# Expert loop with a gated layer behind it: weight conversions and sums issued with lags of steps, in three to four buffers

## The chip, the cores and the metric

One core of a Trainium2 chip runs the program alone. The metric is the device time of one execution in microseconds, the median of the runs. TensorE is PE in the profile (PEld: its weight loads), VectorE is DVE, ScalarE is ACT, GpSimd is POOL, SyncE is SP, which issues nearly all DMAs. PEclk is the granted TensorE clock.

## The reference, cut to what matters

```python
x = attention(q, k, v, f_logit)           # (3072, 384), gated linear attention
# experts: one per token (argmax of the logits), 8 experts, 384 -> 1024 -> 384
for e in range(8):
    h = np.maximum(x[mask] @ w1[e], 0.0)
    out[mask] = gate_w[mask, None] * (h @ w2[e])
x = out
# gated layer, 384 -> 1536 -> 384
a = x @ w_a
b = x @ w_b
return (a * b @ w_out).astype(np.float32)
```

`w_a`, `w_b` and `w_out` arrive as 64-bit floats.

## The kernel before, in words

The program has three stages: attention, the loop over the experts, and the gated layer. All instructions are placed by hand in one program order (each engine takes its own list in order), with the waits on data added by the framework.

**The expert loop** runs steps `s = 0..63` (`NE * FJ`, eight experts of eight blocks of 128 hidden columns). Tokens are sorted by expert; expert 0 has 224 tokens left here, the others 448 down to 384 columns (`CAPS`). A float32 product is three matmuls on a high and a low part (`mm3`). A step has `h_part(s)`: nine matmuls into `ph`, then the Relu `hh` on ACT (L1157) and the low part `hl` on DVE (L1158); and `y_part(s - 1)`: nine matmuls with `hh` and `hl` of the step before into `po` (L1177). After an expert's last block `po` goes to `yT` at an offset known at run time (L1193, L1195). Steps 3 to 5 of each expert turn the next expert's rows (`x_turn`, L1124 to L1128, 84 transposes in the loop). `w_more(s)` runs the jobs that load (`job_load`, L876) and split the expert weights: high part on ACT (L890), low part two thirds on POOL and one third on DVE (L893); two raw tiles, six split tiles.

**The preparation of the gated layer's weights** lies in the same loop. `prep_run(us)` takes operations from one generator, `prep()`, until a credit in us is used, 1.0 per step up to step 7 and 1.5 then; what is left at the last step runs there at once. It has two kinds of work:

- `conv(todo)` turns a piece of a 64-bit weight (768 KB) to float32 with integer operations: a load into `raws` (L910, two buffers in the tile `big`, one piece ahead), Abs on ACT (L916), two tensor_scalars on DVE (L938, L939), then L942 and L947 or L951. Pieces of `w_out` are then split into a high and a low part (L921, L922) and stored to `wost` (L927).
- `combine(w)` keeps the float32 weight of `w_a` or `w_b` in DRAM (`wkeep`, L962) and forms `NR = 15` blocks of 128 x 512, eight of them sums of up to two operations on DVE (L964, L965). For each block: high part on ACT (L1006) and low part on POOL (L1007) into one of two `hilo` buffers, the next block's sums, then the store of the block before to `wst` (L1000). The gated layer multiplies with these fifteen blocks in place of the original ones.

The order is six pieces of `w_out`, six of `w_a`, the sums of a, six of `w_b`, the sums of b. All of it, the converted weight `wf` too, lies in `big` (9216 columns). After step 63 `w_chunk(0..2)` loads the first chunks of `wst`.

**The gated layer** has 392 slots `at`: each a `visit` with six matmuls per block pair on a chunk (L1386), evictions on ACT and DVE (L1389 to L1402), a product and its split (L1363 to L1368), and the output matmuls `pq` with `w_out` (L1415 to L1419), whose pieces `wo_load` reads from `wost` three ahead, in the order 0, 8, 4, 1, 9, 5, 2, 10, 6, 3, 11, 7. Chunks are asked for every four slots, two ahead (`w_chunk(at // 4 + 2)`, L1017).

Of the kernel before, what the change touches and what calls it, by code (L numbers as in the profile page):

```python
# [46 lines left out]
NR = 15  # L47
# [9 lines left out]
def build(tc, I, out, dbg=None):  # L57
# [93 lines left out]
    with tc.manual_schedule():  # L151
# [716 lines left out]
        loaded = []  # L868

        def job_load(s):  # L870
# [28 lines left out]
        hilo_o = big[:, 7680:9216].bitcast(F32R).rearrange("p (i j d) -> p i j d", i=2, j=2)  # L899
# [3 lines left out]
        def conv_load(n, w, c):  # L903
            raw = raws[n % 2].bitcast(I32)
# [5 lines left out]
            SP.dma_start(out=raw.rearrange("p (k f) -> p k f", k=src.shape[1]), in_=src)  # L910

        def conv(todo):
            halves = lambda n: [raws[n % 2].bitcast(I32).rearrange("p (f two) -> p f two", two=2)[:, :, i] for i in range(2)]

            def start(n):
                A.activation(out=ct.bitcast(F32), in_=halves(n)[1].bitcast(F32), func=ACTF.Abs)  # L916

            def rest(n):
                c = todo[n][1]
                src = halves(n)[0].bitcast(F32).rearrange("p (j d) -> p j d", j=2)  # L920
                A.activation(out=hilo_o[:, 0], in_=src, func=ACTF.Copy)  # L921
                G.tensor_tensor(out=hilo_o[:, 1], in0=src, in1=hilo_o[:, 0].bitcast(F32), op=ALU.subtract)  # L922

            def store(n):
                c = todo[n][1]
                for i in range(2):
                    SP.dma_start(out=wost[2 * c:2 * c + 2, :, i].rearrange("j p d -> p j d"), in_=hilo_o[:, i].bitcast(F32))  # L927

            last = lambda n, w: 0 <= n < len(todo) and todo[n][0] == w
            conv_load(0, *todo[0])  # L930
            yield 1.5
            yield 1.5
            start(0)
            for n, (w, c) in enumerate(todo):
                if n + 1 < len(todo):
                    conv_load(n + 1, *todo[n + 1])
                r0, r1 = halves(n)
# [5 lines left out]
                if last(n - 1, 2):  # L943
                    store(n - 1)
                yield 0.95
                if w == 2:
                    V.scalar_tensor_tensor(out=r0, in0=r1, scalar=-1073741824, in1=r0,  # L947
                                           op0=ALU.bitwise_and, op1=ALU.bitwise_xor)
                else:
                    as3 = lambda t: t.rearrange("p (k f) -> p k f", k=KC)  # L950
                    V.scalar_tensor_tensor(out=wf.bitcast(I32)[:, :, c * 256:(c + 1) * 256], in0=as3(r1), scalar=-1073741824,  # L951
                                           in1=as3(r0), op0=ALU.bitwise_and, op1=ALU.bitwise_xor)
                if n + 1 < len(todo):
                    start(n + 1)
                if w == 2:
                    rest(n)
                yield 0.95
            if last(len(todo) - 1, 2):
                store(len(todo) - 1)

        def combine(w):
            SP.dma_start(out=wkeep[w], in_=wf)  # L962
            blk = lambda m, k: wf[:, k, m * 512:(m + 1) * 512]
            two = lambda out, x, y, op=ALU.subtract: V.tensor_tensor(out=out, in0=x, in1=y, op=op)  # L964
            neg = lambda out, x, y: V.scalar_tensor_tensor(out=out, in0=x, scalar=-1.0, in1=y, op0=ALU.mult, op1=ALU.subtract)  # L965
            T0, T1 = tmps
            plan = (
                (14, blk(0, 2), ()),
                (8, blk(0, 1), ()),
                (13, T0, ((two, T0, blk(0, 1), blk(1, 0)),)),  # L970
                (0, blk(1, 0), ()),
                (9, T1, ((two, blk(0, 2), blk(0, 2), blk(0, 0)), (two, T1, blk(1, 0), blk(0, 2)))),
                (3, blk(2, 0), ()),
                (11, blk(0, 2), ((two, blk(0, 2), blk(0, 2), blk(2, 0)),)),
                (6, blk(1, 2), ()),
                (4, blk(0, 0), ((two, blk(0, 0), blk(0, 0), blk(0, 1)), (two, blk(0, 0), blk(0, 0), blk(2, 0), ALU.add))),
# [5 lines left out]
                (2, T0, ((two, T0, blk(0, 2), blk(1, 2), ALU.add), (two, T0, T0, blk(2, 2), ALU.add))),  # L982
            )

            def sums(i):
                if i < NR:
                    for op, *args in plan[i][2]:
                        op(*args)
                    return 0.7 * max(1, len(plan[i][2]))
                return 0.3  # L990

            def store(i):
                late, half, pos = AT[plan[i][0]]
                src = hilo[i % 2].bitcast(F32).rearrange("p t i c -> p t (i c)")
# [7 lines left out]
            yield sums(0)  # L1002
            for i in range(NR):
                as4 = lambda t: t.rearrange("p (t c) -> p t c", t=4)
                src, to = as4(plan[i][1]), hilo[i % 2]
                A.activation(out=to[:, :, 0], in_=src, func=ACTF.Copy)  # L1006
                G.tensor_tensor(out=to[:, :, 1], in0=src, in1=to[:, :, 0].bitcast(F32), op=ALU.subtract)  # L1007
                cost = sums(i + 1)
                if i:
                    store(i - 1)  # L1010
                yield cost
            store(NR - 1)
# [6 lines left out]
        def prep():  # L1019
            yield from conv([(2, c) for c in range(6)] + [(0, c) for c in range(6)])  # L1020
            yield from combine(0)
            yield from conv([(1, c) for c in range(6)])
            yield from combine(1)

        prep_ops = prep()
        credit = [0.0]

        def prep_run(us):
            credit[0] += us
            while credit[0] > 0:  # L1030
                try:
                    credit[0] -= next(prep_ops)
                except StopIteration:
                    credit[0] = -1e9
# [253 lines left out]
        for s in range(NE * FJ):  # L1288
# [67 lines left out]
        def wo_load(n):  # L1356
            if n < NQF:
                SP.dma_start(out=WO[n % 4].bitcast(F32), in_=wost[fseq(n)[1]])
# [101 lines left out]
        for at in range(8 * (NTT * NU + 1)):  # L1460
# [237 lines left out]
```

## Time and profile before

| | |
|---|---|
| median of 3 runs | 928.13 us (927.87 to 934.37) |
| the execution in the profile | 922.55 us, its span 920.8 us |
| PE, DVE, ACT, POOL busy | 790.6, 601.2, 418.8, 412.6 us |
| granted TensorE clock, mean | 0.943 of full |
| DMA | 231.54 MB, mean 251 GB/s |

The span goes from the first to the last instruction. Busy shares are means over the three stages, which have different limits; a stage is read from windows of its own: a row of a window has its start and end, its length, the busy us of each engine with its instructions in brackets, then the granted clock, the busy share of the DMA engines and the rate. Steps are found in the trace by the Relu (L1157), one per step.

### The profile page before, as it was taken

The numbers are of one execution on the slowest core, as the hardware profiler recorded it, in microseconds if no ns is written. First come the engines' busy times: TensorE is split into PE (matmuls) and PEld (weight loads), VectorE is DVE, ScalarE is ACT, GpSimd is POOL, SyncE is SP. The second block draws the span as 40 slices with busy tenths as digits, with TensorE's granted clock in tenths as the row PEclk, the third lists the DMA queues.
The fourth block names the chain that finished last, engine by engine and source line by source line (L and its number), as shares of the span: only waits on it lengthen the run. The fifth ranks groups of instructions, "written<-read, shape, count | busy, mean of one in ns | idle before, by whom it ended". The sixth has DMA issues, their size and how long they took to land.

```text
span 920.8 us, 16764 instructions
## 1 busy us (share of the span) xinstructions
PE 790.6 (86%) x6354; PEld 753.4 (82%) x6354; DVE 601.2 (65%) x993; ACT 418.8 (45%) x889; POOL 412.6 (45%) x394
## 2 busy tenths in 40 slices
PE   7999999878676474887655999999999999999996
PEld 5899899767665473887544999999999999999995
DVE  7999974876555353576481776676676676676652
ACT  5999945543434242534341353443443343443431
POOL 6667843554224453444351252452452452552423
PEclk8999999999979677999786999999999999999998
DMA  7988628787645646654758888987988988988982
GB/s 273 347 280 285 232 96 243 231 265 236 182 146 182 186 128 188 194 199 177 175 146 290 317 304 295 328 315 287 342 301 291 333 299 290 333 307 295 332 307 101
DMA packets 83328, 231.54 MB, mean 251 GB/s; under 512 B 10634, under 2 KB 42232, under 8 KB 76712
## 3 DMA queue, kind: packets, MB, share of 16 engines
q1 hardware_dynamic: 79879, 220.81, 70.8%
q0 software_dynamic: 3072, 9.56, 2.7%
q8 instruction: 52, 0.85, 0.4%
q14 instruction: 37, 0.30, 0.1%
q10 hardware_dynamic: 288, 0.02, 0.0%
HBM read 192.95 MB, written 37.42 MB: 250 GB/s over the span
## 4 chain that ended last, share of the span: by engine, by line
PE 42%; DVE 21%; DMA 13%; issue 13%; POOL 6%; ACT 3%; SPq 1%; ACTq 0%; DVEq 0%; POOLq 0%
PE pv L1386 19%; DMA wst<-big 7%; PE pw L1386 5%; PE pq L1419 4%; PE pq L1415 4%; PE pq L1417 4%; POOL w L893 4%; DMA raw<-moe_w 3%; DVE Rt L242 3%; DVE Bt L231 2%; DVE qc L250 2%; DVE big L1402 2%; DVE big L1363 2%; DMA wost<-big 2%; DVE a L1276 1%
## 5 line engine op out<-in xcount | busy, mean ns | idle before, releaser
L1368 POOL TENSOR_TENSOR w<-big,w 128x512 fp32r<-128x512 f32 x72 | 94.7, 1329 | 205.6 <-ACT w L1367 193.1
L1177 PE MATMUL po<-hh,w 128*128 128x224 f32 (+7 forms) x384 | 92.1, 377 | 71.6 <-ACT hh L1157 71.4
L1386 PE MATMUL pv<-w,w 128*128 128x256 f32 x912 | 135.6, 284 | 15.5 <-DMA w<-wst 13.7
L1386 PEld LDWEIGHTS pv<-w,w 128*128 128x128 f32 x912 | 127.0, 190 | 19.0 <-issue 14.1
L1402 DVE TENSOR_TENSOR big<-big,pv 128x512 f32<-128x512 f32 x144 | 98.2, 682 | 62.5 <-PE pv L1386 61.8
L1177 PEld LDWEIGHTS po<-hh,w 128*128 128x128 f32 x384 | 71.3, 204 | 80.8 <-ACT hh L1157 77.1
L893 POOL TENSOR_TENSOR w<-raw,w 128x512 fp32r<-128x512 f32 x48 | 81.7, 1730 | 87.1 <-ACT w L890 87.1
L1386 PE MATMUL pv<-a,w 128*128 128x256 f32 x816 | 120.2, 281 | 0.3
L1386 PEld LDWEIGHTS pv<-a,w 128*128 128x128 f32 x816 | 113.6, 188 | 2.0 <-DVE big L1396 1.2
L1419 PE MATMUL pq<-raw,w 128*128 128x384 f32 x288 | 97.2, 338 | 1.0 <-POOL w L1368 1.0
L1415 PE MATMUL pq<-raw,w 128*128 128x384 f32 x288 | 97.3, 338 | 0.0
L1417 PE MATMUL pq<-raw,w 128*128 128x384 f32 x288 | 96.9, 337 | 0.0
L1158 DVE SCALAR_TENSOR_TENSOR hl<-ph,hh 128x224 fp32r<-128x224 f32 (+7 forms) x64 | 35.4, 556 | 79.2 <-ACT hh L1157 78.9
L1396 DVE TENSOR_TENSOR big<-big,pv 128x256 f32<-128x256 f32 x96 | 40.3, 420 | 53.6 <-PE pv L1386 51.9
L1007 POOL TENSOR_TENSOR big<-big 128x512 fp32r<-128x512 f32 x30 | 42.0, 1404 | 73.5 <-ACT big L1006 68.1
L1134 PE MATMUL ph<-a,w 128*128 128x224 f32 (+7 forms) x192 | 68.5, 357 | 0.0
L1135 PE MATMUL ph<-a,w 128*128 128x224 f32 (+7 forms) x192 | 67.8, 353 | 0.0
L1136 PE MATMUL ph<-a,w 128*128 128x224 f32 (+7 forms) x192 | 67.3, 351 | 0.0
L1363 DVE TENSOR_TENSOR big<-big 128x512 f32<-128x512 f32 x72 | 65.4, 935 | 1.7
L1367 ACT ACTIVATE w<-big 128x512 fp32r<-128x512 f32 x72 | 44.8, 633 | 34.1 <-DVE big L1363 34.1
L1177 PE MATMUL po<-hl,w 128*128 128x224 f32 (+7 forms) x192 | 51.3, 380 | 9.8 <-DVE hl L1158 9.8
L1006 ACT ACTIVATE big<-big 128x512 fp32r<-128x512 f32 x30 | 18.9, 629 | 86.5 <-DMA wst<-big 81.9
(266 smaller groups left out, 1755.3 us busy)
## 6 DMA issues: line engine op xcount, KB each, us to landing
w<-wst SPq DMA_DIRECT2D x49, 1024.0 KB, 6.7
w<-wst SPq DMA_DIRECT2D x49, 896.0 KB, 5.5
raw<-wost SPq DMA_DIRECT2D x72, 384.0 KB, 5.2
raw<-moe_w SPq DMA_DIRECT2D x32, 768.0 KB, 6.3
qkf<-qkf SPq DMA_DIRECT2D x20, 768.0 KB, 6.2
wst<-big SPq DMA_DIRECT2D x24, 512.0 KB, 6.4
vx<-vx SPq DMA_DIRECT2D x24, 192.0 KB, 7.4
big<-moe_w_out SPq DMA_DIRECT2D x6, 768.0 KB
```

Source lines behind the costliest of these rows:

```text
L893: (G if i < NPOOL else V).tensor_tensor(out=wt[:, 1, f], in0=raw[:, f], in1=wt[:, 0, f].bitcast(F32), op=ALU.subtract)
L1134: T.matmul(out=out, lhsT=wh, rhs=xh, start=first, stop=False)
L1135: T.matmul(out=out, lhsT=wl, rhs=xh, start=False, stop=False)
L1136: T.matmul(out=out, lhsT=wh, rhs=xl, start=False, stop=last)
L1177: T.matmul(out=OS[e][k], lhsT=w[:, j % 4, k * 128:(k + 1) * 128], rhs=x, start=(j == 0 and w is wh and x is hh), stop=(j == FJ - 1 and x i ...
L1363: V.tensor_tensor(out=a, in0=a, in1=b, op=ALU.mult)
L1368: G.tensor_tensor(out=g[:, 1], in0=a, in1=g[:, 0].bitcast(F32), op=ALU.subtract)
L1386: T.matmul(out=out, lhsT=wt, rhs=xt_, start=first and j == 0, stop=j == 2, skip_group_check=True)
L1402: V.tensor_tensor(out=o, in0=o, in1=bank, op=ALU.subtract)
L1415: T.matmul(out=q, lhsT=gh, rhs=wh, start=(f == 0), stop=False)
L1417: T.matmul(out=q, lhsT=gh, rhs=wl, start=False, stop=False)
L1419: T.matmul(out=q, lhsT=gl, rhs=wh, start=False, stop=(f == F2J - 1))
```

## The change

The preparation is rewritten as two generators, `combines()` and `conv()`, that `prep_run(at, us)` runs side by side, at the start of `w_more` instead of behind it; budgets are 1.1 and 1.8 per step, without a carried credit. What has a lag is put into `due` and issued when its step comes.

- Three buffers (`part[3..5]` of `big`) take loads as soon as they are free; a piece is ready for its Abs three steps after its load was issued. The split of a `w_out` piece comes one step after its conversion, its store two.
- `w_a` in float32 (`wfs[0]`) lies in columns 1920 to 3455 of the tiles `yT`, its two temporaries in columns 1408 to 1919: the expert outputs reach them only with the experts 4 and 3. So `w_b` can be converted into `big` while a's sums run, with one buffer until a's sums are done.
- In the sums, a block's split comes one step after its sums, the store one step after that, in three `hilo` buffers for a and four for b; a buffer is taken again at the earliest three steps after. Low parts of the blocks that need no sum go to DVE, the others stay on POOL.
- The order is three pieces of `w_out`, `w_a`, `w_b`, and the other three of `w_out`, which run on into the gated layer (`prep_run` at every third slot, budget 1.0). `w_chunk(0..2)` is issued from step 61 on.
- A raw tile of an expert weight is loaded anew in the step after its job ended (`freed`), and `job_load` runs first in `w_more`.

```diff
         def job_load(s):
-            while jobs and len(loaded) < 2:
+            while jobs and len(loaded) < 2 and (not freed or freed[0] <= s):
+                if freed:
+                    freed.pop(0)
...
-        wf = big[:, 0:KC * FF2].rearrange("p (k f) -> p k f", k=KC)
-        raws = [big[:, 6144:7680], big[:, 4608:6144]]
-        hilo = [big[:, o:o + 1024].bitcast(F32R).rearrange("p (t i c) -> p t i c", t=4, i=2) for o in (7680, 4608)]
-        tmps = [big[:, 8704:9216], big[:, 5632:6144]]
+        wfs = [lambda k: yT[k][:, NT + DM - FF2:NT + DM], lambda k: big[:, k * FF2:(k + 1) * FF2]]
+        tmps = [[yT[i][:, 1408:1920] for i in range(2)], [yT[i][:, NT + DM - 512:NT + DM] for i in range(2)]]
+        part = [big[:, o:o + 1536] for o in range(0, 9216, 1536)]
+        hilo = [big[:, o:o + 1024].bitcast(F32R).rearrange("p (t i c) -> p t i c", t=4, i=2) for o in (4608, 5632, 6656, 7680)]
+        free = {i: 0 for i in (3, 4, 5)}
+        waiting = [(w, c) for w in (2, 0, 1, 2) for c in ((0, 2, 4) if w == 2 else range(6))]
+        waiting[-3:] = [(2, 1), (2, 5), (2, 3)]
...
+        def loads():
+            while waiting:
+                at = sorted((f, i) for i, f in free.items()
+                            if f <= now[0] and (i == 5 or waiting[0][0] != 1 or phase[0] >= 2))
+                if not at or (waiting[0] == (2, 1) and phase[0] < 4):
+                    return
+                i = at[0][1]
+                free[i] = 1e9
+                conv_load(part[i], *waiting[0])
+                ready.append((now[0] + 3, i) + waiting.pop(0))
...
+                A.activation(out=ct.bitcast(F32), in_=r1.bitcast(F32), func=ACTF.Abs)
+                yield 0.5
...
+                    defer(1, split)
+                    defer(2, store)
+                    take(i, 2)
+                    if n >= 15:
+                        for _ in range(4):
+                            yield 9.0
...
+                    for k in range(KC):
+                        if w == 1 and k:
+                            continue
...
+                        V.scalar_tensor_tensor(out=o, in0=one(r1), scalar=-1073741824, in1=one(r0),
+                                               op0=ALU.bitwise_and, op1=ALU.bitwise_xor)
+                    take(i, 1)
...
-            SP.dma_start(out=wkeep[w], in_=wf)
+            for k in range(KC):
+                SP.dma_start(out=wkeep[w, :, k], in_=wfs[w](k))
...
+            def split(i):
+                src, to = as4(plan[i][1]), hilo[i % nh]
+                A.activation(out=to[:, :, 0], in_=src, func=ACTF.Copy)
+
+                def low(eng):
+                    eng.tensor_tensor(out=to[:, :, 1], in0=src, in1=to[:, :, 0].bitcast(F32), op=ALU.subtract)
+
+                if plan[i][2]:
+                    low(G)
+                else:
+                    tail.append((0.8, lambda: low(V)))
+                defer(1, lambda: store(i))
...
+            can = [0] * nh
             for i in range(NR):
+                while now[0] < can[i % nh]:
+                    yield None
+                for op, *args in plan[i][2]:
+                    op(*args)
+                    yield 0.7
+                defer(1, lambda i=i: split(i))
+                can[i % nh] = now[0] + 3
+                yield 0.1
...
+        def prep_run(at, us):
+            now[0] = at
+            for d in [d for d in due if d[0] <= at]:
+                due.remove(d)
+                d[1]()
+            us -= sum(t[0] for t in tail)
+            loads()
+            for g in streams:
+                while us > 0:
+                    cost = next(g, None)
+                    if cost is None:
+                        break
+                    us -= cost
+            while tail:
+                tail.pop(0)[1]()
...
         def w_more(s):
+            job_load(s)
             w_start(s, 0)
             if w_next():
+                freed.append(s + 1)
                 w_start(s, 0)
-                w_next()
-            job_load(s)
+                if w_next():
+                    freed.append(s + 1)
...
+            prep_run(s, 1.1 if s < FJ else 1.8)
             w_more(s)
             if 1 <= s <= 3:
                 next(count_ops)
-            if s >= 2:
-                prep_run(1.0 if s < 8 else 1.5)
...
-            if s == NE * FJ - 1:
-                prep_run(1e9)
-                for h in range(3):
-                    w_chunk(h)
...
+            if at % 3 == 2:
+                prep_run(NE * FJ + at // 3, 1.0)
```

## Rows read from the trace of the kernel before

**Rows 1.** The page's 40 slices of the span: tenths busy, and clock granted.

```profile
PE   7999999878676474887655999999999999999996
...
PEclk8999999999979677999786999999999999999998
```

**Rows 2.** Windows of the loop; PE, PEld, DVE, ACT, POOL, PEclk, DMA share, GB/s.

```profile
143.00:168.60 25.60, 22.70 (x185) 21.72 (x183) 15.15 (x37) 15.19 (x38) 10.20 (x10) 1.00 0.71 216
...
168.60:233.90 65.30, 50.81 (x238) 44.64 (x236) 43.88 (x50) 30.19 (x50) 33.12 (x19) 0.95 0.84 262
...
233.90:339.30 105.40, 67.46 (x323) 63.06 (x324) 54.73 (x65) 37.59 (x72) 41.77 (x27) 0.84 0.54 165
...
339.30:386.30 47.00, 30.85 (x151) 28.72 (x149) 20.69 (x28) 16.75 (x32) 19.33 (x13) 0.82 0.66 194
...
386.30:470.70 84.40, 63.51 (x322) 59.67 (x320) 54.77 (x75) 34.40 (x69) 36.02 (x23) 0.92 0.56 165
...
470.70:494.10 23.40, 6.00 (x28) 5.20 (x28) 11.77 (x21) 5.51 (x14) 10.63 (x5) 0.67 0.61 180
```

**Rows 3.** Waits from 143 to 500 us: in total, times, longest.

```profile
ACT big L1006 <- DMA wst<-big: 81.9, 16, 16.5
...
PEld po L1177 <- ACT hh L1157: 77.1, 20, 12.7
...
ACT ct L916 <- DMA big<-moe_w_a: 33.7, 4, 15.3
...
ACT ct L916 <- DMA big<-moe_w_b: 27.0, 4, 8.7
...
ACT ct L916 <- DMA big<-moe_w_out: 16.5, 4, 8.0
...
PE pv L1386 <- DMA w<-wst: 13.7, 1, 13.7
```

**Rows 4.** Timeline of ACT: start, us, what, count, idle before and releaser.

```profile
145.71 0.81 ACT L1157 ACTIVATE hh<-ph 128x224 fp32r<-128x224 f32 x2
...
257.71 0.89 ACT L916 ACTIVATE ct<-big 128x768 f32<-128x768 f32 x1 [15.27 <-DMA big<-moe_w_a]
...
304.72 0.63 ACT L1006 ACTIVATE big<-big 128x512 fp32r<-128x512 f32 x1 [16.53 <-DMA wst<-big]
```

**Rows 5.** Waits of SP's own list of transfers, 143 to 500 us.

```profile
SPq L1000 <- POOL big L1007: 82.8, 25, 12.3
SPq L876 <- DVE w L893: 64.4, 12, 15.1
```

**Rows 6.** The line that stores wst (L1000), 143 to 500 us.

```profile
DMA to landing us min/median/max: 3.5/4.4/13.3
```

**Rows 7.** Single lines on DVE from 143 us on: duration ns min/median/max.

```profile
L938 DVE TENSOR_SCALAR ct<-ct x18: 542/552/1646, 161.0 to 422.7; 128x768 f32<-128x768 f32 x18
...
L942 DVE SCALAR_TENSOR_TENSOR big<-big,ct x18: 942/959/2050, 163.3 to 423.8; 128x768 int32<-128x768 int32 x18
...
L951 DVE SCALAR_TENSOR_TENSOR big<-big x12: 943/1448/2051, 227.4 to 428.3; 128x768 int32<-128x768 int32 x12
...
L964 DVE TENSOR_TENSOR big<-big x24: 679/992/1782, 289.6 to 479.0; 128x512 f32<-128x512 f32 x24
```

**Rows 8.** Transfers in the window 143 to 500 us.

```profile
DMA packets 44294, 69.59 MB, mean 195 GB/s; under 512 B 5847, under 2 KB 31447, under 8 KB 43762
```

**Rows 9.** Windows at the start of the gated stage, columns as in rows 2.

```profile
494.00:519.00 25.00, 23.87 (x160) 22.64 (x161) 15.43 (x33) 9.35 (x19) 3.21 (x3) 0.90 0.92 355
519.00:545.00 26.00, 26.00 (x195) 25.98 (x194) 16.93 (x31) 10.10 (x23) 11.06 (x12) 1.00 0.83 289
```

**Rows 10.** Windows with TensorE at full clock, columns as in rows 2.

```profile
140.00:150.00 10.00, 10.00 (x91) 9.85 (x89) 5.26 (x19) 4.93 (x15) 2.96 (x5) 1.00 0.74 216
...
370.00:380.00 10.00, 8.36 (x48) 7.88 (x47) 4.73 (x9) 3.82 (x5) 5.98 (x4) 1.00 0.92 268
```

**Rows 11.** Chain of waits: start, us, what; four transposes.

```profile
337.45 0.56 PE pt L1124 x4
```

More of the change, by code (lines that the diff above doesn't have):

```diff
@@ L894, in job_run, with defer, halves, conv_load @@
                                                       op=ALU.subtract)
-        wf = big[:, 0:KC * FF2].rearrange("p (k f) -> p k f", k=KC)
-        raws = [big[:, 6144:7680], big[:, 4608:6144]]
-        hilo = [big[:, o:o + 1024].bitcast(F32R).rearrange("p (t i c) -> p t i c", t=4, i=2) for o in (7680, 4608)]
-        hilo_o = big[:, 7680:9216].bitcast(F32R).rearrange("p (i j d) -> p i j d", i=2, j=2)
-        tmps = [big[:, 8704:9216], big[:, 5632:6144]]
-        WR = [wrs[:, i * 2048:(i + 1) * 2048].rearrange("p (r i c) -> p r i c", r=8, i=2) for i in range(3)]
-        def conv_load(n, w, c):
-            raw = raws[n % 2].bitcast(I32)
+        blocks = lambda t: (lambda m, k: t(k)[:, m * 512:(m + 1) * 512])
+        wfs = [lambda k: yT[k][:, NT + DM - FF2:NT + DM], lambda k: big[:, k * FF2:(k + 1) * FF2]]
+        tmps = [[yT[i][:, 1408:1920] for i in range(2)], [yT[i][:, NT + DM - 512:NT + DM] for i in range(2)]]
+        part = [big[:, o:o + 1536] for o in range(0, 9216, 1536)]
+        hilo = [big[:, o:o + 1024].bitcast(F32R).rearrange("p (t i c) -> p t i c", t=4, i=2) for o in (4608, 5632, 6656, 7680)]
+        WR = [wrs[:, i * 2048:(i + 1) * 2048].rearrange("p (r i c) -> p r i c", r=8, i=2) for i in range(3)]
+        now = [0]
+        due, tail = [], []
+        free = {i: 0 for i in (3, 4, 5)}
+        waiting = [(w, c) for w in (2, 0, 1, 2) for c in ((0, 2, 4) if w == 2 else range(6))]
+        waiting[-3:] = [(2, 1), (2, 5), (2, 3)]
+        ready = []
+        phase = [0]
+        stored = set()
+        def defer(n, fn):
+            due.append((now[0] + n, fn))
+        def halves(raw):
+            return [raw.bitcast(I32).rearrange("p (f two) -> p f two", two=2)[:, :, i] for i in range(2)]
+        def conv_load(raw, w, c):
             if w == 2:
@@ L909, in conv_load @@
                 src = src[:, :, c * 512:(c + 1) * 512]
[L910 to L937, printed above, removed]
@@ new lines, in conv_load @@
+            SP.dma_start(out=raw.bitcast(I32).rearrange("p (k f) -> p k f", k=src.shape[1]), in_=src)
+        def loads():
[8 more added lines that the diff above has]
+                ready.append((now[0] + 3, i) + waiting.pop(0))
@@ L938, in conv, with take @@
+        def take(i, n):
+            free[i] = now[0] + n
+        def conv():
+            for n in range(18):
+                while not ready or now[0] < ready[0][0]:
+                    yield None
+                at, i, w, c = ready.pop(0)
+                raw = part[i]
+                r0, r1 = halves(raw)
+                A.activation(out=ct.bitcast(F32), in_=r1.bitcast(F32), func=ACTF.Abs)
+                yield 0.5
                 V.tensor_scalar(out=ct.bitcast(F32), in0=ct.bitcast(F32), scalar1=C0, scalar2=None, op0=ALU.max)
@@ L957, in conv, with split @@
-                yield 0.95
-            if last(len(todo) - 1, 2):
-                store(len(todo) - 1)
+                    to = part[n if n < 3 else 5].bitcast(F32R).rearrange("p (i j d) -> p i j d", i=2, j=2)
+                    src = r0.bitcast(F32).rearrange("p (j d) -> p j d", j=2)
+                    def split(to=to, src=src):
+                        A.activation(out=to[:, 0], in_=src, func=ACTF.Copy)
+                        G.tensor_tensor(out=to[:, 1], in0=src, in1=to[:, 0].bitcast(F32), op=ALU.subtract)
@@ new lines, in store @@
+                    def store(to=to, c=c):
+                        stored.update((2 * c, 2 * c + 1))
+                        for h in range(2):
+                            SP.dma_start(out=wost[2 * c:2 * c + 2, :, h].rearrange("j p d -> p j d"), in_=to[:, h].bitcast(F32))
+                    defer(1, split)
[4 more added lines that the diff above has]
+                            yield 9.0
+                else:
+                    for k in range(KC):
+                        if w == 1 and k:
+                            continue
+                        if w == 0:
+                            one = lambda t: t[:, k * 256:(k + 1) * 256]
+                            o = wfs[0](k)[:, c * 256:(c + 1) * 256].bitcast(I32)
+                        else:
+                            one = lambda t: t.rearrange("p (k f) -> p k f", k=KC)
+                            o = big[:, 0:KC * FF2].bitcast(I32).rearrange("p (k f) -> p k f", k=KC)[:, :, c * 256:(c + 1) * 256]
+                        V.scalar_tensor_tensor(out=o, in0=one(r1), scalar=-1073741824, in1=one(r0),
+                                               op0=ALU.bitwise_and, op1=ALU.bitwise_xor)
+                    take(i, 1)
@@ L965, in combine @@
             neg = lambda out, x, y: V.scalar_tensor_tensor(out=out, in0=x, scalar=-1.0, in1=y, op0=ALU.mult, op1=ALU.subtract)
[L966 removed]
+            T0, T1 = tmps[w]
             plan = (
                 (14, blk(0, 2), ()),
+                (13, T0, ((two, T0, blk(0, 1), blk(1, 0)),)),
                 (8, blk(0, 1), ()),
[L970 removed]
                 (0, blk(1, 0), ()),
@@ L1000, in store @@
                         SP.dma_start(out=dst, in_=src[:, lo:hi])
-            yield sums(0)
+            can = [0] * nh
             for i in range(NR):
[L1004 to L1012, printed above, removed]
+                while now[0] < can[i % nh]:
+                    yield None
+                for op, *args in plan[i][2]:
[4 more added lines that the diff above has]
+                yield 0.1
+            until = now[0] + 3
+            while now[0] < until:
+                yield None
         def w_chunk(h):
@@ L1017, in w_chunk, with combines @@
                 SP.dma_start(out=WR[h % 3][:, 0:n].bitcast(F32), in_=wst[h % (2 * NU), :, 0:n])
-        def prep():
-            yield from conv([(2, c) for c in range(6)] + [(0, c) for c in range(6)])
+        def combines():
+            while phase[0] < 1:
+                yield None
             yield from combine(0)
-            yield from conv([(1, c) for c in range(6)])
-            yield from combine(1)
[L1025 to L1034, printed above, removed]
+            phase[0] = max(phase[0], 2)
+            free[3] = free[4] = now[0]
+            while phase[0] < 3:
+                yield None
+            free[3] = free[4] = free[5] = 1e9
+            yield from combine(1)
+            free[4] = now[0]
+            phase[0] = 4
+            while now[0] <= NE * FJ - 4:
+                yield None
+            for h in range(3):
+                w_chunk(h)
+        streams = [combines(), conv()]
+        def prep_run(at, us):
[13 more added lines that the diff above has]
+                tail.pop(0)[1]()
+        loads()
         running = []
```

36 lines of the change are left out of this document (16 added, 20 removed).

## The prediction

> **What bounds the kernel now.** I read the page's slices first, to find the part where TensorE is not full. In the 40 slices PE stands at 9 from slice 23 to 39; from 8 to 22 it falls as low as 4, and the granted clock falls to 6 and 7 tenths there (means over a slice of its two levels, 1.2 and 2.4 GHz) [rows 1]. That part is the loop over the experts, 64 steps s of 18 matmuls each (plus 84 transposes), from 145.7 to 494.1 us. So the time to be had is in this loop, and what is taken from it comes off the end, since everything behind is a full TensorE.
>
> Next the windows, cut where the Relu of steps 8, 20, 37, 45 and 61 starts and where the first gated matmul starts [rows 2]. The lengths are 22.9 (from the first Relu at 145.7), 65.3, 105.4, 47.0, 84.4 and 23.4 us, 348.3 in all with rounding. In the third, 105.4 us for 17 steps, no engine is busy for more than 67.5 us, and the DMA share is 0.54: nothing is full there, so it is waits.
>
> The waits name them [rows 3]. ACT stood 81.9 us before L1006 for DMAs that store wst, and 33.7 + 27.0 + 16.5 us before L916 for loads of w_a, w_b and w_out: 159.1 us. ACT takes its list in order, so the Relu of the next step stands behind: PE's weight loads for po waited 77.1 us in one row for L1157. The timeline of ACT has the first Relu at 145.71 and two such places: 16.53 us before an L1006, 15.27 us before an L916 [rows 4]. At the end of the loop PE waited another 13.7 us for the first weight chunk [rows 3]. 159.1 + 13.7 = 172.8 us of waits stand against a loop whose matmuls need about 200 (below): the two make up 348 nearly whole. SP's own list waits too, 82.8 us for POOL's L1007 before it can store, 64.4 us for DVE's L893 before it can load [rows 5].
>
> **The change part by part.** I walk the two new generators step by step with the costs they yield (budget 1.1 up to step 7, then 1.8). Three loads go out before step 0. Abs of the first w_out piece is at step 3, of w_a's six pieces at steps 9, 11, 13, 14, 16, 18; a's sums run from step 20 to 33, their last store is at step 35; w_b's Abs are at 23, 29, 35 (one buffer) and 40, 41, 43; b's sums run from 45 to 56, the last store at 58. The chunks for the gated stage are issued at step 61, and three of six w_out pieces are converted at steps 63, 69 and 75, that is, the last two beside the gated stage.
>
> *Waits for loads (L916), 77.2 us.* Each Abs now stands three steps or more behind its load: 3 steps at some 3.3 us are 10 us, against the worst seen, 15.3 us [rows 4], which contains SP's own delay. I take the gain at nearly all.
>
> *Waits for stores (L1006), 81.9 us.* The split comes one step after the sums, the store one after that, and the buffer is written again two steps after its store (6.6 us). A store lands 3.5 to 13.3 us after issue, median 4.4 [rows 6]. By the walk a's items go in bunches of about three, ten bunches for both weights. A bunch is 1.57 MB, so at the rate below the third lands about 3.3 us after the first: 7.7 us, 1.1 late. Ten bunches: 11 us at most, less where PE has a step of matmuls queued. I charge 9.
> The Trainium skill's page "DMA: Bandwidth & Descriptors" (section "Latency and other measured facts") gives HBM's latency as 0.2 us on average and 2 us at high load. It speaks against this step, for the change closes the gaps in the queue; an estimate by that page is up to 1.8 us more on each bunch, 18 us. This trace has the spread of landings but not their cause. The sum does not use it; rival 1 is priced from rows.
>
> *SP.* Stores and raw loads move one step later, past the op they waited for, and job_load runs before the jobs. What is moved past: the three early loads (2.4 MB) stand ahead of the rows of expert 1, needed at step 3. They cost 2.4 MB at 0.31 MB/us, 7.5 us, of which the 22.9 us stretch has idle DMA for about 7 (share 0.71) [rows 2]. I charge nothing; uncovered it is 7.5.
>
> *DVE.* Seven lows of fifteen move from POOL to DVE, 14 in all. The nearest row is L964, the same shape, 0.68 to 1.78 us, median 0.99: +14 us [rows 7]. Three w_out pieces leave: two tensor_scalars at 0.55, 0.96, 1.45, so 3.5 us each, -10.5. The loop's DVE time was 201.0 (the sum of the six windows [rows 2]), so 204. With every one of 15 conversions and 40 sums and lows at its shortest it is 169; with all at their longest (7.4 us a piece, 1.78 a sum) 279. I take 204, the mean that is there under the same neighbour. w_a's last step in three instructions instead of one adds 12 instruction starts, a few us inside those bounds. The moved lows bring a new wait: each stands on DVE behind its own hi copy on ACT, and up to three of these are issued in a row at 0.63 us [rows 4], so the last low starts 1.9 us after the Relu at the earliest. Behind it on DVE stand the job's low and the next hl, for which PE waits. In seven or eight such steps that is 8 to 10 us of DVE standing; none of it shows if PE has a step queued. POOL loses fourteen ops and was busy 151 of 351 us (the six windows); it is no bound.
>
> *DMA.* 69.6 MB cross in this window [rows 8]; without three w_out loads and stores (6 x 0.786 MB) 64.9. The 65.3 us stretch moved 262 GB/s at a share of 0.84 [rows 2], 312 if full: 208 us. By the gated stage's start, 355 at 0.92 [rows 9], it is 168. I take 208, the same kinds of transfer.
>
> *PE.* At 400 columns and full clock 48 matmuls took 8.36 us, 0.174 each; at expert 0's 224 columns 91 in 10.0, 0.110 [rows 10]. Scaled by columns the steps cost 1.98, 3.51, 3.38, 3.26, 3.19, 3.13, 3.07 and 3.01 us from expert 0 to 7: 196 us. Four transposes alone took 0.56 [rows 11], so 84 are 12 at most, 6 behind matmuls: 202. The lower clock of the slices with waits [rows 1] goes with them.
>
> *Sum.* The largest need of each stretch: steps 0 to 7, DMA 22 (6.9 MB); 8 to 19, PE 44 with transposes; 20 to 36, DMA 66 (three w_b pieces of 0.786 MB, 2.4 MB of wkeep, 7.9 of sums, 8.5 raw pieces, two sets of rows: 20.6 MB) against PE 58; 37 to 44, PE 27; 45 to 60, PE 52; 61 to the first visit 14, with DVE's x_first. Together 225. To that 9 for the bunches and 8 for the new wait on DVE, which has little to spare against PE in the second and third stretches: 242. 348.3 - 242 = 106 us less.
>
> *The gated stage.* Here PE is full, so nothing can be won. Two pieces are added beside it, 3.1 MB of loads and stores in its first 25 us, 8 to 9 us of DMA at 355 GB/s, where the share leaves 2 free, and 4.4 in the next 26 us [rows 9]. What hides it is that chunks are asked for two ahead. Bounds 0 and 9; I take 4, between them. Their DVE work (two times 3.5 us) lies beside 15.4 busy of 25 and costs nothing unless it delays an eviction. The store of the first late w_out piece goes out at slot 6, and the output matmuls ask for it some 30 slots later.
>
> Net 106 - 4 = 102. The execution in the profile took 922.55 us, 1.75 over its span of 920.8, so it would be 820.5. The median of the runs shown is 5.6 above this execution, so 928.13 - 102 = 826.
>
> **Rivals.**
> *1. The waits for DMA come back.* If the filled queue stretches landings to the 13.3 us that the trace already has [rows 6], each of ten bunches waits 6.7 us: 67, 9 of it counted, and a queued step hides about 1 of each: +48, 874 us. For it: the queue will be busy nine tenths of the time. Against: the median is 4.4, and 13.3 is the worst of 36. By the Trainium skill's latency figure from that page it would be 844, to which I give 0.06 of this rival's chance.
> *2. DVE becomes the bound* at its longest durations: a loop of 279 instead of 242, 863 us. For it: L951 is at 1.45 in the median, not 0.94, beside a busy POOL [rows 7]. Against: POOL gets less work.
> *3. The change does not do what it says.* Lags are counted in steps of the program, not in time, and SP may still hold a load behind a store whose low part is late, as its 82.8 us show [rows 5]. Then ACT waits as before and only part of the 13.7 us at the end is won: 922.
> *4. Slower.* The DMA rate, not the waits, sets the loop's length. In the two stretches with wst stores the rate is 165 GB/s [rows 2]. If the queue cannot do better with loads and stores mixed, 64.9 MB at 178 GB/s (between that 165 and 192, the mean of the six windows) take 365 us, and 4.7 MB moved into the gated stage, uncovered, 15 more: 380 against 348, 959 us. It decides below 195 GB/s (64.9 MB in 348 - 15 us). Against it: 262 in the second window and a share of 0.54 where the rate is 165.
>
> **How the numbers follow.** Forecast 0.69 (its own range 800 to 850), rival 1 0.14, rival 2 0.08, rival 3 0.04, rival 4 0.05. Below 800 the loop would have to run at the 225 of the sum or under, which I hold for 0.08 of the forecast's share. The range 796 to 876 takes in rivals 1 and 2 and leaves out 3 and 4 and the tails, under two in ten. A measurement of this kernel can tell about 1% from no change. Faster by over 1%: 0.69 + 0.14 + 0.08 = 0.91; within: 0.04; slower: 0.05.
>
> **What would show it.** In the profile after: ACT's waits before Abs and before the hi copy for DMA together under 30 us; the loop 225 to 265 us long; the granted clock in it near 1; DVE busy about 204 and the DMA share near 0.85 in it; no 13.7 us before the first gated matmul; the gated stage within 9 us of before. I am wrong if the loop is over 290 us (then see whether DMA or DVE stands ahead of the Relu), or if the gated stage is longer by more than 9.

## The result, and the profile after

The kernel after the change takes 842.78 us (median of four runs, 841.32 to 843.84) against 929.38 for the kernel before on the same chip: a ratio of 0.906, interval 0.902 to 0.910. The forecast was 826, in a range of 796 to 876. The medians differ by 86.6 us, the two executions in the profiles (922.55 and 843.84) by 78.7, for the one of before lies 6.8 under this median and the one of after 1.1 over its own; the lengths below are of these two.

The page's slices, answering to [rows 1] (40 slices, now of 842 us, so each 21 us long):

```profile
PE   7899989599988899889878999999999999999995
...
PEclk9999999799999989989999999999999999999999
```

Outside the first slices, which belong to the attention stage, two slices of TensorE are left at 5: the eighth, at the start of the loop, and the last, where the program ends (6 before). The windows of the loop and of the first 51 us of the gated stage, cut at the same steps as [rows 2] and [rows 9] (PE, PEld, DVE, ACT, POOL, clock, DMA share, GB/s; the seventh row is the whole loop):

```profile
143.00:180.80 37.80, 26.91 (x197) 25.86 (x196) 18.95 (x44) 17.02 (x42) 11.37 (x10) 0.82 0.77 224
...
180.80:229.30 48.50, 45.71 (x233) 40.50 (x233) 47.20 (x63) 28.54 (x49) 23.32 (x16) 1.00 0.74 238
...
229.30:304.50 75.20, 65.05 (x337) 61.53 (x336) 58.51 (x73) 39.35 (x73) 39.21 (x26) 0.95 0.93 276
...
304.50:334.50 30.00, 28.11 (x156) 26.84 (x154) 19.80 (x29) 16.16 (x28) 12.68 (x8) 1.00 0.71 222
...
334.50:396.30 61.80, 55.29 (x306) 54.34 (x307) 47.90 (x71) 33.76 (x66) 35.32 (x21) 0.94 0.83 232
...
396.30:408.00 11.70, 11.70 (x73) 11.27 (x71) 8.74 (x20) 6.36 (x14) 0.00 (x0) 1.00 1.01 414
...
143.00:404.20 261.20, 228.96 (x1266) 216.71 (x1265) 197.44 (x289) 139.12 (x265) 121.90 (x79) 0.95 0.82 250
...
404.20:429.20 25.00, 19.52 (x135) 17.84 (x133) 16.68 (x32) 9.34 (x18) 3.37 (x2) 0.93 0.88 321
429.20:455.20 26.00, 20.94 (x151) 20.17 (x151) 21.44 (x33) 9.22 (x19) 12.90 (x11) 1.00 0.88 326
```

The first Relu is at 148.5 us, the first gated matmul at 404.2. The stretches, before and after: steps 0 to 7 22.9 and 32.3 us, 8 to 19 65.3 and 48.5, 20 to 36 105.4 and 75.2, 37 to 44 47.0 and 30.0, 45 to 60 84.4 and 61.8, from 61 to the first gated matmul 23.4 and 7.9. So the loop fell from 348.3 to 255.6, by 92.7. From there to the end it is 437.8 us against 426.8: the gated stage grew by 11.0. The loop also began 2.8 us later, in code that is the same; in the twelve variants of the changed kernel that follow it began at 144.8 to 146.5, so that is one execution's. 92.7 - 11.0 - 2.8 = 78.9, within rounding the difference of the two spans, 78.8.

The waits in the loop of the kernel after (143 to 404.2 us; total, times, longest), answering to [rows 3]:

```profile
PEld po L1248 <- ACT hh L1228: 18.2, 8, 5.6
...
ACT big L1028 <- DMA wst<-big: 15.3, 5, 6.6
ACT w L893 <- DMA raw<-moe_w: 12.5, 7, 6.6
...
ACT w L887 <- DMA raw<-moe_w: 11.6, 2, 11.2
...
DVE big L1031 <- ACT big L1028: 9.9, 2, 7.2
PEld pt L1195 <- DMA yT<-slots: 9.6, 1, 9.6
...
ACT ct L949 <- DMA big<-moe_w_b: 0.8, 1, 0.8
```

L1028 is the hi copy (L1006 before), L949 the Abs (L916), L1228 the Relu (L1157). ACT's 159.1 us of waits for these DMAs are 16.1. One line is new: PE's transposes of expert 1's rows wait 9.6 us for their load. Another kind grew: ACT waits 24.1 us for the raw pieces of the expert weights (L887, L893), 11.2 of them once in the first stretch. Before it waited 7.2 for them (L884, L890), from 143 to 500 us:

```profile
ACT w L884 <- DMA raw<-moe_w: 4.2, 2, 2.7
ACT w L890 <- DMA raw<-moe_w: 3.0, 2, 2.5
```

### The profile page after: what moved, and what is told of

It reads as the page before. It is cut to its first block, busy times and chain, and to the rows that moved or that the text cites. A ratio compares the mean times of both kernels' runs of the same rounds, so it can differ in the third digit from the quotient of the medians.

```text
span 842.0 us, 16799 instructions
## 1 busy us (share of the span) xinstructions
PE 777.7 (92%) x6354; PEld 743.7 (88%) x6354; DVE 609.2 (72%) x1019; ACT 420.9 (50%) x889; POOL 392.1 (47%) x380
## 5 line engine op out<-in xcount | busy, mean ns | idle before, releaser
L1435 POOL TENSOR_TENSOR w<-big,w 128x512 fp32r<-128x512 f32 x72 | 96.4, 1354 | 194.8 <-ACT w L1434 182.3
L1469 DVE TENSOR_TENSOR big<-big,pv 128x512 f32<-128x512 f32 x144 | 98.3, 683 | 62.5 <-PE pv L1453 62.4
L896 POOL TENSOR_TENSOR w<-raw,w 128x512 fp32r<-128x512 f32 x48 | 76.7, 1626 | 60.4 <-ACT w L893 56.5
L1248 PE MATMUL po<-hh,w 128*128 128x224 f32 (+7 forms) x384 | 84.0, 355 | 17.0 <-ACT hh L1228 16.4
L1248 PEld LDWEIGHTS po<-hh,w 128*128 128x128 f32 x384 | 68.8, 196 | 20.5 <-ACT hh L1228 18.2
L1205 PE MATMUL ph<-a,w 128*128 128x224 f32 (+7 forms) x192 | 66.9, 349 | 0.0
L1206 PE MATMUL ph<-a,w 128*128 128x224 f32 (+7 forms) x192 | 66.8, 348 | 0.0
L1207 PE MATMUL ph<-a,w 128*128 128x224 f32 (+7 forms) x192 | 66.7, 347 | 0.0
L1460 ACT ACTIVATE big<-pw 128x256 f32<-128x256 f32 x48 | 18.4, 383 | 77.8 <-PE pw L1453 77.8
L1486 PEld LDWEIGHTS pq<-raw,w 128*128 128x128 f32 x288 | 54.5, 189 | 1.6 <-POOL w L1435 1.6
L1482 PEld LDWEIGHTS pq<-raw,w 128*128 128x128 f32 x288 | 54.4, 189 | 0.3 <-ACT w L1434 0.3
L1484 PEld LDWEIGHTS pq<-raw,w 128*128 128x128 f32 x288 | 54.5, 189 | 0.0
```

Source lines behind the costliest of these rows:

```text
L896: (G if i < NPOOL else V).tensor_tensor(out=wt[:, 1, f], in0=raw[:, f], in1=wt[:, 0, f].bitcast(F32), op=ALU.subtract)
L1205: T.matmul(out=out, lhsT=wh, rhs=xh, start=first, stop=False)
L1206: T.matmul(out=out, lhsT=wl, rhs=xh, start=False, stop=False)
L1207: T.matmul(out=out, lhsT=wh, rhs=xl, start=False, stop=last)
L1248: T.matmul(out=OS[e][k], lhsT=w[:, j % 4, k * 128:(k + 1) * 128], rhs=x, start=(j == 0 and w is wh and x is hh), stop=(j == FJ - 1 and x i ...
L1435: G.tensor_tensor(out=g[:, 1], in0=a, in1=g[:, 0].bitcast(F32), op=ALU.subtract)
```

## The experiments

Lengths are read from each run's own profile, ratios are to the kernel before on the run's own chip; so times of different groups of runs differ by up to 0.6 per cent for the same kernel. In the runs that leave these stretches as they are (the kernel after, `e1`, `e2`, `e3`, `f1`) steps 20 to 36 take 71.2 to 75.2 us, 37 to 44 29.5 to 34.3, 45 to 60 60.0 to 62.3, the three together 165.5 to 167.1. A smaller difference in one of them is no effect.

**Stores.** `e4`, two hilo buffers in the sums, each taken again after one step in place of three (split and store keep their step each):

```diff
-            nh = 3 + w
+            nh = 2
...
-                can[i % nh] = now[0] + 3
+                can[i % nh] = now[0] + 1
```

> The sums have two hilo buffers, and a buffer is split again in the step in which its store is issued. Theory (the lag and the buffers took away ACT's wait for stores): ACT waits before its hi copy for DMA go from 15 us back to 60 to 80, and the time to 875 to 905 us. Rival (most of the gain came from the load lead and from b's conversion beside a's sums): within 8 us of 842.8.

One execution: 875.4 us. The loop is 299.9 us long, 44.3 more, nearly all in the stretches of the sums, 96.1 and 86.9. Its waits from 143 to 445 us:

```profile
ACT big L1028 <- DMA wst<-big: 86.1, 22, 13.7
...
PEld po L1248 <- ACT hh L1228: 48.4, 11, 11.7
```

ACT's wait for stores is back at 86.1 us (81.9 before the change), a little more than expected, and PE's wait for the Relu rises with it, by 30. The theory holds.

**Loads.** `e5`, the lead of three steps undone:

```diff
-                ready.append((now[0] + 3, i) + waiting.pop(0))
+                ready.append((now[0], i) + waiting.pop(0))
```

> A piece is ready for its Abs in the step in which its load was issued. Theory (the lead of three steps took away ACT's wait for loads): ACT waits before Abs for DMA go from 2.3 us to 50 to 75, and the time from 842.8 to 868 to 893 us. Rival (with three buffers the loads are early enough without it): within 8 us of 842.8.

One execution: 889.3 us, a loop of 316.2, 60.6 more. Its waits from 143 to 463 us:

```profile
PEld po L1248 <- ACT hh L1228: 57.0, 10, 10.9
ACT ct L949 <- DMA big<-moe_w_b: 55.8, 6, 14.6
...
ACT ct L949 <- DMA big<-moe_w_out: 15.6, 2, 12.9
```

71.4 us before the Abs, as the theory had it. Undone one at a time, the two lags give 44.3 and 60.6 us, 104.9 together, more than the 92.7 that the loop won: they overlap, and these loops hold work that the loop after does not. That was not expected: with either edit the preparation is done sooner, in `e5` all of w_out inside the loop, in `e4` the Abs of one late piece at step 61, and the gated stage is 424.9 and 428.4 us long in place of 437.8. The whole time rises by 46.5 us in `e5` and by 32.6 in `e4`.

**The late w_out pieces.** `e2` leaves out the last three pieces altogether; the output matmuls read the other three twice:

```diff
+                if waiting[0] == (2, 1):
+                    waiting.clear()
+                    return
...
-            for n in range(18):
+            for n in range(15):
...
-                assert fseq(n)[1] in stored
-                SP.dma_start(out=WO[n % 4].bitcast(F32), in_=wost[fseq(n)[1]])
+                r = fseq(n)[1]
+                SP.dma_start(out=WO[n % 4].bitcast(F32), in_=wost[r - 2 if (r // 2) % 2 else r])
```

> Leaves out the load, conversion and store of the last three w_out pieces (the output matmuls read the other three twice). Theory (they cost the gated stage what it lost): from the first gated matmul to the end 427 us as before the change, in place of 437.8, and about 832 us in all. Rival (the stage lost its time to something else, such as the earlier start of the chunk loads): over 434 us for the stage, 839 or more in all.

Ratio 0.892 (0.888 to 0.897). The gated stage is 424.5 us, so the pieces cost 13.4. `e3` keeps their DMAs and leaves out their instructions on ACT, DVE and POOL; the output matmuls read as in `e2`:

```diff
-                A.activation(out=ct.bitcast(F32), in_=r1.bitcast(F32), func=ACTF.Abs)
+                run = n < 15
+                if run:
+                    A.activation(out=ct.bitcast(F32), in_=r1.bitcast(F32), func=ACTF.Abs)
...
-                V.tensor_scalar(out=ct.bitcast(F32), in0=ct.bitcast(F32), scalar1=C0, scalar2=None, op0=ALU.max)
...
+                run and V.tensor_scalar(out=ct.bitcast(F32), in0=ct.bitcast(F32), scalar1=C0, scalar2=None, op0=ALU.max)
...
-                    defer(1, split)
+                    run and defer(1, split)
```

> Keeps the loads and stores of the last three w_out pieces, leaves out their work on ACT, DVE and POOL. Theory (the DVE and ACT instructions delay evictions, PE waits for them): nearly all of what the run without the pieces gains is gained here too, the stage at 428 to 431 us, about 834 us. Rival (the DMAs delay the weight chunks): the stage stays at 435 to 438 us, about 842 us.

Ratio 0.902 (0.898 to 0.906), the stage 432.2 us. That fits neither expectation: 7.7 us are the DMAs' and 5.7 the instructions'. The waits of PE at the start of the stage, first in the kernel after (404.2 to 470 us), then in `e3` (401 to 467 us):

```profile
PEld pv L1453 <- DVE big L1469: 7.9, 5, 3.5
...
PE pv L1453 <- DVE big L1469: 6.1, 3, 3.2
...
PE pv L1453 <- DMA w<-wst: 4.1, 2, 2.2
...
PEld pv L1453 <- DVE ct L951: 2.2, 1, 2.2
```

```profile
PE pv L1455 <- DMA w<-wst: 7.1, 4, 3.4
PEld pv L1455 <- issue: 5.9, 2, 3.6
```

With the conversions PE waits for evictions on DVE (L1469), and the longest of these waits stand behind a conversion's shifts; without them what is left are late chunks. The longest in the timeline, on DVE and at PE's weight load:

```profile
427.42 0.95 DVE L955 SCALAR_TENSOR_TENSOR big<-big,ct 128x768 int32<-128x768 int32 x1
...
428.41 1.90 DVE L958 SCALAR_TENSOR_TENSOR big<-big 128x768 int32<-128x768 int32 x1
...
430.89 0.62 DVE L1469 TENSOR_TENSOR big<-big,pv 128x512 f32<-128x512 f32 x1
...
431.57 0.77 PEld L1453 LDWEIGHTS pv<-w,w 128*128 128x128 f32 x6 [3.51 <-DVE big L1469]
```

In the 26 us from 429.2 DVE is busy 21.4 us, against 16.9 in [rows 9], and PE only 20.9.

**The first loads.** `e1` drops the call ahead of the loop, so that the loads go out in step 0:

```diff
-        loads()
-
         running = []
```

> The first three conversion loads are issued in step 0 instead of ahead of the loop, so behind the rows of expert 1 and the raw piece. Theory (they delayed the rows): PE's wait of 9.4 us for yT<-slots and ACT's 11.2 us for raw<-moe_w go, the stretch from the first Relu to step 8 falls from 32.3 us to about 24, and the time from 842.8 to about 835. Rival (the 2.4 MB must pass in this stretch anyway): the wait moves to the first Abs, and the time stays within 3 us of 842.8.

Ratio 0.904 (0.899 to 0.909): neither side is told apart by the time. By the profile the first stretch is 29.2 us, 3.1 less; PE no longer waits for the rows, but ACT waits 7.7 us at the first Abs for w_out, as the rival had it. `f1` puts the loads between, right behind the rows and the raw piece:

```diff
-        loads()
-
         running = []
...
         loaded.extend((-9, n, None, RAW[n]) for n in (4, 5))
+        loads()
```

> Only the first three conversion loads move, to right behind the rows of expert 1 and the raw piece. Theory (their place in the queue is what the first stretch lost): the first stretch falls from 32.3 us to about 25, the others stay, the ratio to the kernel before from 0.906 to about 0.898. Rival (what is won there is lost again by the first expert weights coming late): a ratio of 0.903 or more.

The first stretch is 24.7 us, as expected, and the wait at the first Abs 3.1; the loop is 246.4 us, 9.2 less than after. Its window of the first stretch (columns as above), to be held against 143.00:180.80:

```profile
144.80:169.50 24.70, 20.93 (x156) 20.00 (x156) 16.89 (x39) 14.15 (x35) 10.26 (x7) 0.93 0.94 309
```

The ratio is 0.903 (0.901 to 0.906), the rival's number, though the profile does not have the rival's wait: ACT waits 16.8 us for raw pieces, against 24.1. It lies below the 0.906 of the change, but the intervals overlap and the chips differed (923.95 against 929.38 for the kernel before). The 9.2 us compare the fastest of five executions with the slowest of four. So the shorter first stretch is shown, in the four runs that move these loads there (24.7 to 25.1 us); that it makes a faster kernel is suggested by the profile and not shown by the times.

**wkeep.** `e6` leaves out the copies of the float32 weights (the two `SP.dma_start(out=wkeep...)` lines):

> Leaves out the copies of the float32 weights to wkeep (2 x 2.36 MB, which this input never reads). Theory (they stand in the queue ahead of the first stores of the sums, and ACT's hi copy waits behind them): the stretch from step 20 to 37 falls from 75.2 to about 67 us, that from 45 to 61 from 61.8 to about 54, the time to about 828. Rival (these stretches are bound by DVE and by the length of the matmuls): under 4 us in both together.

Ratio 0.904 (0.901 to 0.907). The stretches of the sums are 69.2 and 59.3 us, 6.0 and 2.5 less, but the one between them grew by 4.2: the three together are 162.8 us, 2.7 less than in any run that leaves them as they are. The loop is 251.2, 4.4 less. So the copies cost the loop some 3 to 4 us where the theory said 16, and not in its way: ACT waits 14.9 us before the hi copy for stores, against 15.3 with the copies. `f3` moves the loads as in `f1` and stores wkeep in six parts, each a step after its conversion:

> The loads moved, and the wkeep copies in six parts, each a step after its conversion. Theory (a copy of 2.36 MB ahead of the first stores delays them): 4 to 8 us less in the stretches of the sums, a ratio near 0.892. Rival (the bytes only move, and the parts have small packets): within 2 us of the run with the loads moved alone.

Ratio 0.903 (0.901 to 0.906), loop 247.6 against 246.4 for `f1`: the rival. Moving the copies gains nothing.

**Bunches.** `f2` moves the loads and lets at most two blocks start per step:

```diff
+            last = [-1, 0]
             for i in range(NR):
+                while last[0] == now[0] and last[1] >= 2:
+                    yield None
+                last[:] = [now[0], last[1] + 1 if last[0] == now[0] else 1]
```

> The loads moved, and at most two blocks of the sums per step instead of up to four. Theory (bunched stores lengthen landings, so ACT's hi copy waits): the stretches of the sums fall by 3 to 4 us each against the run with the loads moved alone, a ratio near 0.890. Rival (their length comes from bytes and matmuls, not from bunching): within 2 us of it.

Ratio 0.905 (0.902 to 0.907); the sums take 74.2 and 63.7 us against 71.2 and 60.0 in `f1`, the three stretches together 167.4 against 165.5. The theory falls: spreading the bunches does not help.

**DVE's share of the low parts.** `e9` gives them all to POOL (`low(G)` in place of the choice):

> All low parts of the sums on POOL, as before the change; DVE has 14 instructions less. Theory (DVE is not the bound; the moved lows cost it some 10 us that lie beside other work): within 4 us of 842.8. Rival (DVE sets the pace of the sums): the stretches of the sums shorter by 5 us or more together. Second rival (POOL's low parts hold up the stores): longer by 5 us or more.

Ratio 0.913 (0.911 to 0.916), just above the change's 0.902 to 0.910. The stretch of a's sums is 0.8 us shorter, that of b's 5.0 longer (66.8 us, POOL busy 43.0 of it, 35.3 in the kernel after), the loop 4.0 longer. That is the second rival in b's sums and not in a's. So DVE does not set the pace of the sums, and by this run the moved instructions pay.

**Budget.** `e7` spends 2.6 per step from step 36 on:

```diff
-            prep_run(s, 1.1 if s < FJ else 1.8)
+            prep_run(s, 1.1 if s < FJ else 1.8 if s < 36 else 2.6)
```

> The step budget is 2.6 from step 36 on, so that b's sums end two steps earlier and the late w_out pieces start three preparation steps earlier: the first is converted before the gated stage, the others nine slots earlier. Theory (the late pieces cost most in the first slots of the gated stage, where chunks are asked for fastest): the stage falls from 437.8 us to 429 to 433, the loop stays within 3 us of 255.6, the time 835 to 838. Rival (their cost is the same wherever they stand, or the loop pays it): within 3 us of 842.8.

Ratio 0.912 (0.908 to 0.916). The gated stage is 434.4 us, 3.4 less, but the loop 262.6, 7.0 more: 2.8, 3.5 and 3.7 in the three stretches from step 37 on, 3.1 less ahead of them. The loop pays for it. `e8` has this budget, the loads of `f1` and the wkeep parts of `f3`:

> Three edits together: the first loads right behind the rows of expert 1 and the raw piece, the wkeep copies in six parts one step after each conversion, and the budget of 2.6 from step 36. Theory: the first stretch 32.3 to about 26 us, the stretches of the sums 75.2 to about 69 and 61.8 to about 55, the gated stage to about 431; the time about 818. Rival (the DMA engines are full over the whole loop, so a copy moved is a copy paid elsewhere): the second stretch grows by what the third and fifth lose, and the time is 830 or more.

Ratio 0.905 (0.902 to 0.909): first stretch 24.9 us, sums 73.7 and 66.3, gated stage 433.9, and 838.5 us in all, as in the rival, though the second stretch did not grow (48.8). Of its three edits only the loads gain.

## Why the prediction was right, and which terms were mis-sized

The mechanism was right: ACT stood in order before its waits for loads and stores with the Relu behind, and the lags take both away. Each undone alone brings its wait back, and 44 and 61 us of the loop (`e4`, `e5`), which also rules out rival 3, that lags in steps would not hold in time. No run undoes the rest of the change by itself (three w_out pieces out of the loop, w_b beside a's sums, chunks asked for from step 61): that the last stretch is 15.5 us shorter because the chunks come early is read from the wait of 13.7 us that is gone, and not tested. The 172.8 us of waits and the 202 of matmuls, which I set against the loop's 348, make 375: part of the waits lay beside matmuls. PE's busy time in the loop's windows fell from 241.3 us to 229.0, at a granted clock of 0.88 before and 0.95 after. Rival 1 has a small part: 15.3 us of waits for stores are left, where I charged 9. By the estimate from the latency in the Trainium skill's page "DMA: Bandwidth & Descriptors" (section "Latency and other measured facts") the time would have been 844, close to the one measured; no run here shows that latency, and the runs place the missing time elsewhere, in the first loads and the gated stage. Rival 4 falls with the rate: 276 GB/s in the stretch that had 165.

The number came nearer than its terms. For the execution in the profile the forecast was 820.5, and it took 843.8, 23.3 more. The forecast of the median then added the 5.6 us by which the median lay above the profiled execution before; after, it lies 1.1 below, and these nearly 7 us are luck.

*What was foreseen.* ACT's waits for these DMAs under 30 us (16.1); DVE about 204 (197.4 from 143 to 404.2 us); DMA share near 0.85 in the loop (0.82 in the same window); the step of each Abs in the loop that the walk names; no wait for the first chunk; the loop between 225 and 265 us (255.6). The granted clock (a mean over the levels 1.2 and 2.4 GHz) came back to 0.94 and over in every stretch but the first.

*The gated stage,* which I put at +4 within 0 and 9, is 13.4 us for the pieces (`e2`), 11.0 against the kernel before: more than 9, which I had named as a sign of being wrong. The failed step is that I charged nothing for their DVE work, which "costs nothing unless it delays an eviction": it does delay evictions, and with the pieces' work on ACT and POOL it costs 5.7 us (`e3`). The share of busy time in a window of 25 us, 15.4, hid that an eviction can stand behind a conversion. I also counted two pieces beside the stage, and there are three: the first has its Abs at 403.3 us, and its DVE work starts as the first gated matmul does. The DMAs cost 7.7, inside the bounds but above the 4 that I took.

*The early loads,* charged at nothing, "uncovered it is 7.5": they were uncovered. PE's 9.6 us for the rows is that wait, and `f1` wins 7.6 us of the stretch. I had set idle DMA time of a whole stretch against a transfer needed at its third step.

*The loop's other stretches.* Against the 225 of my sum the second took 4.5 us more, the third 9.2, the fourth 3.0, the fifth 9.8, the first 10.3, the last 6.1 less; of these 30.7 us I had 17 in reserve. In the second DVE is busy 47.2 of 48.5 us and PE 45.7: for twelve steps DVE is about as full as rival 2 had it, but its conversions are not at their longest (L955 0.96 us in the median), and no run lightens DVE there. In the third the sum took the DMA engines for the bound, at 312 GB/s when full; their share is 0.93 at 276, so 297 when full, and at that rate the 20.8 MB of the stretch would take 70 us and not 66. PE's own time was charged too low as well: it is busy 65.1 and 55.3 us in the third and fifth, where the sum had 58 and 52, at a granted clock of 0.95 and 0.94. ACT's waits for raw pieces, 7.5 us in the third, I had not charged at all. The fifth has ACT's longest wait for a store. The timeline around it, SP's issues and the hi copy on ACT:

```profile
344.86 1.03 SPq L879 DMA_DIRECT2D raw<-moe_w  x2
...
347.12 13.15 SPq L1047 DMA_DIRECT2D wst<-big  x7
...
356.29 0.63 ACT L1028 ACTIVATE big<-yT 128x512 fp32r<-128x512 f32 x1 [6.58 <-DMA wst<-big]
```

Two raw pieces go out ahead of the stores (seven up to 360.3 us), and the hi copy starts 9 us after the first store was issued, having waited 6.6. My term for the bunches counted the stores alone and not the raw pieces in the same queue; that these lengthened the wait is not shown, for no run moves them. What else makes this stretch longer than its matmuls stays open: neither spreading the blocks (`f2`, 63.7 us) nor moving wkeep (`f3`, 60.6) shortened it against `f1` (60.0).

*DVE's moved low parts:* +14 us and a new wait of 8 in the sum. The line's DVE instructions in the kernel after (ns, min/median/max):

```profile
L1031 DVE TENSOR_TENSOR big<-yT,big x7: 679/693/1780, 235.0 to 283.4; 128x512 fp32r<-128x512 f32 x7
L1031 DVE TENSOR_TENSOR big<-big x7: 675/693/1786, 343.4 to 379.0; 128x512 fp32r<-128x512 f32 x7
```

A low part took 0.69 us in the median, not 0.99. The new wait is there, L1031 for L1028, 9.9 us in all, but at two places and not seven or eight, 7.2 of it behind ACT's long wait for a store. With all of them on POOL the loop is 4.0 us longer (`e9`), so the sum charged 8 where the move, all told, gains.

## What to carry to other kernels

An engine that takes its list in order should not meet a wait for a DMA that its neighbour issued in the same step: issue the load, the use and the store steps apart, with a buffer for each step between; here undoing the one made the loop 44 us longer, undoing the other 61, and the whole 33 and 47 us (one execution each). When such work is moved, look at what its transfers stand ahead of in the queue and when that is needed, not at the idle share of the stretch. Work moved beside a stage whose main engine is full is not free because the helping engine has idle time: price it by what it puts in front of the evictions.

## What was not expected of the hardware

The 11.7 us around the end of the loop moved 414 GB/s at a DMA share of 1.01, over the 386 that [rows 9] gave for full engines, while the stretch of a's sums, with a share of 0.93, moved 276: the share says how long the engines are busy, not how much they carry. The packets differ, in the windows 229.3 to 304.5 and 396.3 to 408 us:

```profile
DMA packets 13870, 20.79 MB, mean 276 GB/s; under 512 B 715, under 2 KB 10462, under 8 KB 13865
```

```profile
DMA packets 1089, 4.84 MB, mean 414 GB/s; under 512 B 111, under 2 KB 111, under 8 KB 832
```

Three in four are under 2 KB in the first, one in ten in the second. And PE waited for chunks at the start of the gated stage with the share at 0.88, so a share under one is no sign that a transfer is in time.

The same DVE instruction took two durations. Of the twelve L951 of the kernel before ([rows 7]), the six that ran while POOL was idle took 0.94 to 0.96 us, the six beside a POOL instruction 1.94 to 2.05. Not every pair does this: some L964 beside POOL took 0.68.
